# A transformer block on one core: full-height passes for the first gate and up products, and a planner that counts changes of TensorE's tile form

## The chip, the core and the metric

The kernel runs on one core of a Trainium2 chip. The core has five engines that run side by side and meet at semaphores: TensorE (PE in the profile, with its weight loads as PEld), VectorE (DVE), ScalarE (ACT), GpSimd (POOL) and SyncE (SP), which here does nothing but issue transfers. TensorE multiplies a stationary operand, which a weight load puts into its 128x128 array, with a moving operand, and accumulates into the eight banks of PSUM (128 partitions x 512 floats each). The metric is the device time of one execution in microseconds (us), lower is better.

## The reference

x is 2048 tokens of width 448, all in float32. The block is attention with a residual, then a gated feed-forward with a residual:

```python
h  = x + attention(layernorm(x)) @ wo        # 16 heads of 28, scale 28 ** -0.5,
                                             # a query sees itself and the 255 tokens before it
n  = layernorm(h)
h2 = h + (gelu(n @ w_gate) * (n @ w_up)) @ w_down   # 448 -> 1792 -> 448
```

## The kernel before, in words

**Precision.** Most products split each operand into a high part (rounded to the type that TensorE multiplies in one pass) and a low part, and add high x high, high x low and low x high: three passes for a product. ScalarE writes the high parts (`to_hi`), VectorE or GpSimd the low ones (`to_lo`).

**Attention.** There are 16 blocks B, each four heads by 512 queries. For a block, TensorE makes the scores (`scores`, L717), VectorE their row maxima, a small transpose brings the maxima to the keys' side (L748), TensorE makes the scores again transposed (`probs`, L792), ScalarE takes the exponential (L796), GpSimd zeroes what the window excludes (L811), TensorE multiplies with the values (`attend`, L830), `drain` normalises on VectorE and GpSimd, and after every second block `output` (L888) multiplies with wo. Query, key and value projections (L666, L612) of a later group of tokens lie between these steps. The last projections end during block 12, and blocks 13 to 15 are attention's tail.

**Feed-forward.** The 1792 hidden features are seven groups of 256 and the tokens two halves, which makes 14 pieces `m`. The first three pieces (CL = 3) are computed in the plain way, for two times 512 tokens and for gate and up each: twelve turns x = 0 to 11. The other eleven use a scheme of seven products in place of eight on halves of 64 contraction rows, and need no closer look here. All of it is issued as TensorE "slots": a slot is three pairs of passes, each pass on 64 of the 128 rows of the array, the two of a pair on the upper and the lower half at once, into two banks (`cslot` L1123 for the plain turns, `both` L1314 for the others, `down_half` L1388 for the product with w_down). In a plain turn the 448 contraction rows are three chunks of 128 and a rest of 64. `cslot(..., ph, j, banks)` takes half a chunk for each of the two output tiles: with ph = 0 the upper half for one tile and the lower half for the other, with ph = 1 the reverse; j = 3 is the rest. So a turn is three slots in `first` and four in `second`, 42 passes on half the rows. Between the two phases `seen` lets ScalarE read one element of a bank (L1234), which orders the two halves' writes into it. Turns 0 to 2 (kind "gu0", banks 5 and 6, named bank_177 and bank_178) may run while attention's tail is still at work, and turn 3 just after. The others come later.

**Three forms of the array.** In this text form 0 is a pass that uses the array as one piece (all of attention but `attend`, and `output`), form 1 is the pairs on 64 rows, and form 2 is `attend`, which uses four column strips of 32.

**What sets the order.** Nothing is written in the order in which it runs. Every step is an `op` with an engine, a cost, a latency, a key and the data that it reads and writes. `Lists.run` plans them: for each engine it looks for the steps that can start within a small margin of the earliest (EASE), takes the one with the lowest key (`choice`), and books its cost. The instructions stand in each engine's queue in the planned order, and each engine works its queue strictly in that order. The PSUM bank of a step is also given in the plan. All TensorE steps of the feed-forward are chained in program order (`queued`), so that the plan moves only what stands between them and what stands on the other engines. Some 50 constants at the top of the file enter keys: EVICT is how far an emptying of a bank is moved ahead, HASTE how far the splitting of w_down is, WLATE and XLATE how far back the weights and the second half of the tokens are put, XTIME in which half units of the feed-forward the three parts of those tokens are prepared, LAG_T, LAG_P and LAG_V how far maxima, probabilities and values trail the scores.

**Banks emptied.** `copied` and `added` (L1320, L1324) and the gelu of a plain turn (L1137) empty a bank of the feed-forward; a later slot that writes the same bank waits for that.

## Time and profile before

| | |
|---|---|
| median of 3 runs | 714.14 us (714.09 to 714.24) |
| the profiled execution | 714.1 us, its span 712.4 us |
| TensorE busy | 698.2 us, 98% of the span |
| VectorE, ScalarE, GpSimd busy | 75%, 58%, 44% |
| granted TensorE clock | 0.999 |
| first plain slot on TensorE; last `output` pass | 271.2 us; 329.2 us |

The span runs from the first to the last instruction; the time holds 1.7 us more, which lies around it. A row of the timeline merges neighbouring instructions of one kind: start, duration, engine, line, operation, output from input, rows used*columns, shape, and how many. Passes are pipelined: the recorded durations overlap, so what a row costs TensorE is best read from its start to the start of the next row.

### The profile page before, as it was taken

The page shows a single profiled execution, that of the slowest core. Times are in us where ns is not written, and L with a number is a line of the kernel's source. Part 1 is how long each engine was busy: PE and PEld are TensorE (multiplying, and loading weights), DVE is VectorE, ACT ScalarE, POOL GpSimd, SP SyncE. Part 2 cuts the span into 40 slices and gives each one's busy share as a digit, 9 for nine tenths or more (in the row PEclk, how much of TensorE's full clock was granted, in tenths as well). Part 3 has the DMA queues.
Part 4 walks back from the last instruction along what each step waited for, and adds up shares of the span by engine and source line. Part 5 has one row for each costly group of instructions (what it writes and reads, how often), then busy time and mean ns, then how long its engine had stood idle before and what let it go on. Part 6 is the DMA issues. An engine that isn't in the chain of part 4 may idle for free. (4 is left out here: it accounts for less than half of the span.)

```text
span 712.4 us, 15568 instructions
## 1 busy us (share of the span) xinstructions
PE 698.2 (98%) x5598; PEld 589.1 (83%) x5598; DVE 536.8 (75%) x1233; ACT 415.9 (58%) x917; POOL 312.7 (44%) x426
## 2 busy tenths in 40 slices
PE   8999999999999999999999999999999999999997
PEld 7887877787888876668787888788899999888996
DVE  7976779887787878838488678995755867877764
ACT  7748586876676675776454546645434545546431
POOL 5613553644465446441025876534403556556000
PEclk9999999999999999999999999999999999999999
DMA  8897967887778775305875866404303563443102
GB/s 310 271 289 208 276 169 192 223 233 212 190 182 250 212 225 143 95 12 129 231 190 172 233 188 190 133 18 135 90 4 109 175 191 114 131 156 87 41 14 104
DMA packets 104693, 116.27 MB, mean 163 GB/s; under 512 B 44632, under 2 KB 82392, under 8 KB 104040
## 3 DMA queue, kind: packets, MB, share of 16 engines
q1 hardware_dynamic: 104472, 115.17, 56.5%
q8 instruction: 44, 0.72, 0.4%
q14 instruction: 33, 0.27, 0.1%
q10 hardware_dynamic: 144, 0.11, 0.0%
HBM read 84.97 MB, written 44.47 MB: 182 GB/s over the span
## 5 line engine op out<-in xcount | busy, mean ns | idle before, releaser
L721 DVE CUSTOM_DVE_ANT_0 mt<-bank,mt 128x384 bf16<-128x384 f32 (+2 forms) x256 | 127.0, 527 | 32.3 <-PE bank L717 30.2
L796 ACT ACTIVATE pp<-bank 128x384 f32<-128x384 f32 (+1 forms) x212 | 105.2, 534 | 27.3 <-PE bank L792 18.0
L811 POOL TENSOR_SCALAR_AFFINE_SELECT pp<-pp 128x512 f32<-128x512 f32 x120 | 77.2, 658 | 86.1 <-ACT pp L796 83.8
L666 PE MATMUL bank<-xT 128*128 128x512 f32 x308 | 95.3, 400 | 0.0
L1314 PE MATMUL bank<-xT,proj 64*128 64x512 f32 x735 | 95.2, 388 | 0.0
L1314 PEld LDWEIGHTS bank<-xT,proj 64*128 64x128 f32 x735 | 77.7, 184 | 7.1 <-ACT raw L1320 0.2
L792 PE MATMUL bank<-rq,rk 104*128 104x384 f32 (+2 forms) x352 | 81.8, 307 | 0.7 <-ACT pp L796 0.6
L717 PE MATMUL bank<-rk,rq 84*128 84x384 f32 (+2 forms) x256 | 79.8, 342 | 0.7 <-DVE mx L721 0.7
L1388 PE MATMUL bank<-proj,gh 64*128 64x448 f32 x624 | 72.9, 363 | 2.0 <-ACT e L1234 2.0
L792 PEld LDWEIGHTS bank<-rq,rk 104*128 104x128 f32 x352 | 58.6, 189 | 15.8 <-ACT pp L796 6.9
L1388 PEld LDWEIGHTS bank<-proj,gh 64*128 64x128 f32 x624 | 61.7, 184 | 7.4 <-ACT e L1234 2.7
L1405 DVE TENSOR_TENSOR hres<-bank,hres 128x448 f32<-128x448 f32 (+1 forms) x113 | 62.9, 611 | 6.4 <-PE bank L1388 6.4
L1234 ACT ACTIVATE e<-bank 1x1 f32<-1x1 f32 x145 | 22.8, 157 | 68.0 <-PE bank L1388 48.0
L1183 POOL TENSOR_TENSOR xn<-proj 128x384 f32<-128x384 f32 (+1 forms) x36 | 37.2, 1039 | 56.6 <-DMA proj<-gu 42.9
L666 PEld LDWEIGHTS bank<-xT 128*128 128x128 f32 x308 | 55.6, 189 | 7.2 <-DVE proj L387 0.5
L717 PEld LDWEIGHTS bank<-rk,rq 84*128 84x128 f32 x256 | 46.7, 189 | 13.6 <-DVE mx L721 5.0
L1123 PE MATMUL bank<-xT,proj 64*128 64x512 f32 x420 | 53.5, 396 | 0.0
L384 ACT ACTIVATE rq<-bank 8x512 fp32r<-8x512 f32 x64 | 37.7, 589 | 26.2 <-PE bank L748 25.2
L1314 PE MATMUL bank<-xo,proj 64*128 64x512 f32 x366 | 48.5, 390 | 2.9 <-DVE v L1324 1.9
L387 DVE TENSOR_TENSOR proj<-proj 128x448 fp32r<-128x448 f32 (+2 forms) x42 | 31.0, 743 | 25.0 <-ACT proj L384 22.8
L612 PE MATMUL bank<-proj,xT 128*128 128x448 f32 (+1 forms) x220 | 48.0, 333 | 0.0
L1123 PEld LDWEIGHTS bank<-xT,proj 64*128 64x128 f32 x420 | 38.2, 184 | 10.4 <-issue 2.6
(175 smaller groups left out, 1420.7 us busy)
## 6 DMA issues: line engine op xcount, KB each, us to landing
rk<-k SPq DMA_DIRECT2D x44, 336.0 KB
rq<-q SPq DMA_DIRECT2D x32, 336.0 KB
gu<-in_gu_dram SPq DMA_DIRECT2D x18, 480.0 KB
proj<-gu SPq DMA_DIRECT2D x24, 288.0 KB
q<-proj SPq DMA_DIRECT2D x12, 448.0 KB
proj<-down SPq DMA_DIRECT2D x22, 224.0 KB
proj<-gu SPq DMA_DIRECT2D x24, 192.0 KB
k<-proj SPq DMA_DIRECT2D x9, 448.0 KB
```

The source lines that it names most:

```text
L384: nc.scalar.activation(dst, src, AF.Copy)
L612: op("pe", mm(224 * n), 0.29 if n == 1 else 0.38, key + a / 16, lambda a=a, h=h, wb=wb, xb=xb: nc.tensor.matmul(bank[b.k][:, 0:224 * n], x ...
L666: op("pe", mm(512) + 0.002, 0.403, key, lambda a=a, h=h, wb=wb, xb=xb: nc.tensor.matmul(bank[b.k], wqk[m][:, h, wb, :], xT[:, xb, cc * 128 ...
L717: nc.tensor.matmul(bank[b.k][:, o:384], rq[u][0:3 * DH, j, i * 128:i * 128 + 128], rk[u][0:3 * DH, j, m0 * 128:(i + 3) * 128], start=True, ...
L721: nc.vector.tensor_tensor_reduce(junk[s % 2][:, o:384], bank[b.k][:, o:384], mask[:, o:384], 1.0, -BIG, OP.add, OP.max, mx[:, i, j:j + 1])
L792: nc.tensor.matmul(bank[b.k][:, n * i:n * i + n], rk[u][0:104, j + i, m * 128:m * 128 + 128], rq[u][0:104, j + i, lo * 128:(hi + 1) * 128] ...
L796: nc.scalar.activation(pp[:, j:j + G, o * 128:o * 128 + n], bank[b.k][:, 0:G * n].rearrange("p (g t) -> p g t", g=G), AF.Exp, scale=SCALE)
L811: nc.gpsimd.affine_select(a, a, pattern=[[0, 4], [-cm, 128]], compare_op=op_, fill=0.0, base=0, channel_multiplier=cm)
L1123: nc.tensor.matmul(bank[banks[side ^ ph].k], cwbuf[n % 4][0]()[HALF[side], o:o + 128], carea(c, xl, j, side), start=not ph and not j and n ...
L1314: nc.tensor.matmul(bank[b.k], w, xarea(u.cp, xl, xs, side)[:, xk], start=p in (1, 2, 5) and not k and not t, stop=t == 2, tile_position=(6 ...
L1388: nc.tensor.matmul(bank[banks[q].k][:, 0:D], h[oh][0]()[HALF[x], q * 128:q * 128 + 128], d[wh][0]()[HALF[x]], start=not ph and not y and n ...
L1405: op("dve", 0.07 + w * 0.463 / D, 0.163 + w * 0.463 / D, key, lambda: nc.vector.tensor_tensor(hres[:, t, c0:c0 + w], bank[b.k][:, c0:c0 + ...
```

## The change

1. In turns 0, 1 and 2 (FULL = 3) the three chunks of 128 rows are no longer cut into halves. `cfull` makes three passes over all 128 rows into one bank, for each of three chunks and two output tiles: 18 passes in form 0 in the place of 36 on half the rows. The rest of 64 rows stays a `cslot` in form 1 (`range(3, 4)` in `second`), and the two `seen` of such a turn fall away. The other turns are as before.
2. Every step carries a `mode`, the form of its passes (0, 1 or 2). `choice` now plans a TensorE step whose form differs from that of the step before no earlier than TURN after TensorE comes free (0.19 for going to form 0, 0.09 for going to form 1 or 2). The delay is booked in the plan; which of the steps that could start goes first is still decided by the key.
3. The planned costs of `probs` and `attend` are altered, and 21 constants, which move steps in the plan; the first lines of the diff show those that matter below.

```diff
-EDGE = 9
+EDGE = 12
+FULL = 3
-XTIME = (6, 6, 8)
+XTIME = (6, 7, 8)
-XLATE = 0
-HASTE = 260
-WLATE = 65
+XLATE = 125
+XSTEP = 60
+HASTE = 300
+WLATE = 110
-XADD = ('dve', 'dve', 'dve', 'dve')
-XLO = ('dve', 'dve', 'dve', 'dve', 'pool')
+XADD = ('dve', 'pool', 'dve', 'dve')
+XLO = ('pool', 'dve', 'dve', 'dve', 'dve')
-EVICT = 15
+EVICT = 30
+TURN = (0.19, 0.09, 0.09)
...
-                    found.append((t, o, got))
+                    late = max(t, free[e] + TURN[o.mode]) if e == "pe" and o.mode != mode else t
+                    found.append((late, o, got, t))
...
-            return min((f for f in found if f[0] <= t0), key=lambda f: (f[1].key, f[0]))
+            return min((f for f in found if f[3] <= t0), key=lambda f: (f[1].key, f[0]))[:3]
...
-            cost = G * (n / 2400 + 0.009)
+            cost = G * max(n / 2400 + 0.009, 0.1)
...
-        cost = 0.33 + n * 0.214
-        op("pe", cost, cost + 0.2, 16 * B + LAG_P + ORDER[ms[-1]] + LAG_V, go, r, (), b, tag="att")
+        cost = 0.157 + n * 0.214
+        op("pe", cost, cost + 0.2, 16 * B + LAG_P + ORDER[ms[-1]] + LAG_V, go, r, (), b, tag="att", mode=2)
...
+        key0 = key
         for k in parts:
+            key = key0 + (0 if cp else XSTEP * k)
...
+    def cfull(key, n, c, k, i, banks):
+        reads = [t for l in range(2) for side in range(2)
+                 for t in (*cwtok(n, l, 384 * i + 128 * k, 128, side), *ctok(c, l, k, side))]
+
+        def go():
+            for t, (wl, xl) in enumerate(((0, 0), (0, 1), (1, 0))):
+                o = 896 * (1 - wl) + 384 * i + 128 * k
+                nc.tensor.matmul(bank[banks[i].k], cwbuf[n % 4][0]()[:, o:o + 128], carea(c, xl, k, 2),
+                                 start=not k and not t, stop=False, skip_group_check=True)
+        queued(op("pe", 0.7, 0.87, key, go, reads, (), banks[i]))
...
         def first(x):
             m, c, ty, banks = turns[x]
             key = ckey(x)
+            if x < FULL:
+                for j in range(6):
+                    cfull(key + j, 2 * m + ty, c, j // 2, j % 2, banks)
+                return
...
-            for b in banks:
-                seen(key, b)
-            for j in range(4):
+            if x >= FULL:
+                for b in banks:
+                    seen(key, b)
+            for j in range(0 if x >= FULL else 3, 4):
                 cslot(key + 2 * j, 2 * m + ty, c, 1, j, banks)
```

On TensorE, over block 15 in attention's tail, the plain slots of L1123 stood one at a time between single probability passes of L792 (bank_177 and bank_178 are the plain turns' banks, bank_174, 175 and 179 those of the probabilities; each pair of L1123 rows stands three times):

```order
L792 MATMUL bank_179<-rq_190,rk_188 128x384
L1123 MATMUL bank_178<-xT,proj 128x512
L1123 MATMUL bank_177<-xT,proj 128x512
...
L792 MATMUL bank_174<-rq_190,rk_188 128x384
L1123 MATMUL bank_178<-xT,proj 128x512
L1123 MATMUL bank_177<-xT,proj 128x512
...
L792 MATMUL bank_175<-rq_190,rk_188 128x384
L792 MATMUL bank_179<-rq_190,rk_188 128x384
```

In the changed kernel the same place on TensorE reads so, with L798 for the probabilities and L1143 for `cfull`:

```order
L798 MATMUL bank_179<-rq_190,rk_188 128x256 x2
L1143 MATMUL bank_177<-xT,proj 128x512 x3
L798 MATMUL bank_174<-rq_190,rk_188 128x256 x2
L1143 MATMUL bank_178<-xT,proj 128x512 x3
L798 MATMUL bank_175<-rq_190,rk_188 128x384
L798 MATMUL bank_179<-rq_190,rk_188 128x384
L1143 MATMUL bank_177<-xT,proj 128x512 x3
```

Three full passes now stand after each one or two probability passes, all in form 0. Counted over the whole of TensorE's queue, the form changes 94 times before and 70 times now: the separate stretches of form 1 ahead of the last `output` are 15 before and 3 now, and the visits to form 2 are 31 in both. From the last `output` passes on, the 3335 passes that follow are the same in the same order, with the same banks, to the end.

On ScalarE, at the end of a plain turn in the feed-forward (bank_174 and bank_175 hold its gate products, L1137 empties them with the gelu, L1234 is `seen`, the L384 rows split weights), before:

```order
L1234 ACTIVATE e_75<-bank_173 1x1
L384 ACTIVATE w_3388<-xn 128x384
L1137 ACTIVATE v<-bank_174 128x512
L384 ACTIVATE proj<-proj 128x448
L1137 ACTIVATE e_3390<-bank_175 128x512
L1234 ACTIVATE e_75<-bank_177 1x1
L1234 ACTIVATE e_75<-bank_179 1x1
```

and in the changed kernel, at the same turn on ScalarE (L1156, L1253 and L390 are the same three lines):

```order
L1156 ACTIVATE v<-bank_174 128x512
L1156 ACTIVATE e_3345<-bank_175 128x512
L1253 ACTIVATE e_75<-bank_177 1x1
L390 ACTIVATE w_3343<-xn 128x128
L1253 ACTIVATE e_75<-bank_179 1x1
L390 ACTIVATE w_3343<-xn 128x384
L390 ACTIVATE proj<-proj 128x448
```

The two emptyings now stand side by side, and the splits of weights behind them.

On VectorE, in a later unit of the feed-forward (L1324 empties a bank, L387 makes low parts, L1342 multiplies gate and up), before:

```order
L387 TENSOR_TENSOR w_3388<-xn,w_3388 128x384
L1342 TENSOR_TENSOR v<-raw,v 128x512
L1324 TENSOR_TENSOR v<-bank_172,v 128x512
L387 TENSOR_TENSOR e_3392<-v,e_3391 128x512
L1324 TENSOR_TENSOR v<-bank_175,v 128x512
```

and now, at the same unit on VectorE (L1361, L1343 and L393 are the same three lines):

```order
L1361 TENSOR_TENSOR v<-raw,v 128x512
L393 TENSOR_TENSOR w_3343<-w_3343 128x384
L393 TENSOR_TENSOR w_3343<-xn,w_3343 128x384
L393 TENSOR_TENSOR e_3347<-v,e_3346 128x512
L1343 TENSOR_TENSOR v<-bank_172,v 128x512
L1343 TENSOR_TENSOR v<-bank_175,v 128x512
```

The low part of the activation moved from between the two emptyings to ahead of both. Over the whole program ScalarE has 6 instructions fewer (the `seen` of three turns), VectorE 5 fewer and GpSimd 5 more (token preparation), and SyncE issues the same transfers.

More of the change, by code (lines that the diff above doesn't have):

```diff
@@ L93 @@
     __slots__ = ("eng", "cost", "lat", "key", "fn", "deps", "users", "left", "banks", "port", "ready", "start", "fin",
-                 "size", "tag")
+                 "size", "tag", "mode")
 class Bank:
@@ L109, in __init__, with op @@
         self.ops, self.seen, self.open, self.all = [], {}, {}, {}
-    def op(self, eng, cost, lat, key, fn, r=(), w=(), bank=None, port=False, size=0, tag=None, after=(), part=None):
+    def op(self, eng, cost, lat, key, fn, r=(), w=(), bank=None, port=False, size=0, tag=None, after=(), part=None, mode=0):
         o = Op()
-        o.eng, o.cost, o.lat, o.key, o.fn, o.port, o.size, o.tag = eng, cost, lat, key, fn, port, size, tag
+        o.eng, o.cost, o.lat, o.key, o.fn, o.port, o.size, o.tag, o.mode = eng, cost, lat, key, fn, port, size, tag, mode
         o.deps, o.users, o.ready, o.start = set(after), [], 0.0, None
@@ L221, in run @@
                 dmas.append(t + lat)
-            if e == "pe" and t < SLOW:
-                cost, lat = 2 * cost, lat + cost
+            if e == "pe":
+                mode = o.mode
+                if t < SLOW:
+                    cost, lat = 2 * cost, lat + cost
             free[e] = t + cost
@@ L1315, in go @@
                                      stop=t == 2, tile_position=(64 * side, 0), skip_group_check=True)
-        queued(op("pe", 0.69, 0.86, key, go, reads, (), [x[3] for x in two]))
+        queued(op("pe", 0.69, 0.86, key, go, reads, (), [x[3] for x in two], mode=1))
     def copied(key, buf, b):
@@ L1393, in down_half @@
             queued(op("pe", 3 * mm(D), 3 * mm(D) + 0.17, key + j, lambda j=j: go(j, h, d), [h[0][1], h[1][1], *d[0][1], *d[1][1]], (),
[L1394 removed]
+                      [banks[2 * j], banks[2 * j + 1]], mode=1))
             if not ph:
```

31 lines of the change are left out of this document (15 added, 16 removed).

## The prediction

> **What bounds the kernel.** I read the page first, then the chain of waits, then busy time by stretch.
>
> ```profile
> span 712.4 us, 15568 instructions
> PE 698.2 (98%) x5598; PEld 589.1 (83%) x5598; DVE 536.8 (75%) x1233; ACT 415.9 (58%) x917; POOL 312.7 (44%) x426
> ...
> PE 27%; DVE 1%; issue 0%; DVEq 0%
> ```
>
> TensorE is busy for 98% of the span, and the chain that ended last is nearly all TensorE. So the time is the sum of what TensorE issues, and I look for two things: passes that cost more than they should, and waits that the busy share hides because pipelined passes overlap. The stretches below show TensorE's busy time in the first number after the comma; the stretch's length minus that is idle time.
>
> ```profile
> 296.00:329.00 33.00, 32.66 (x263) 23.13 (x262) 18.16 (x45) 23.75 (x49) 12.15 (x19) 1.00 0.13 30
> 329.00:360.00 31.00, 30.07 (x263) 24.40 (x263) 20.22 (x38) 15.01 (x39) 4.53 (x9) 1.00 0.82 206
> 360.00:400.00 40.00, 38.93 (x354) 33.42 (x352) 31.34 (x54) 20.11 (x54) 18.33 (x16) 1.00 0.71 191
> 400.00:440.00 40.00, 37.99 (x338) 33.36 (x337) 34.20 (x48) 24.10 (x59) 27.48 (x27) 1.00 0.71 208
> 440.00:480.00 40.00, 39.02 (x352) 33.45 (x351) 37.96 (x56) 20.61 (x51) 20.54 (x18) 1.00 0.31 90
> 520.00:560.00 40.00, 40.00 (x368) 36.99 (x366) 23.68 (x36) 16.17 (x40) 9.74 (x10) 1.00 0.31 90
> ```
>
> From 329 to 480 us TensorE idles 0.9 + 1.1 + 2.0 + 1.0 = 5.0 us; from 520 to 560 none. In attention's tail (296 to 329) it hardly idles, so a gain there must come from the passes themselves. The timeline of the tail, start by start, shows where:
>
> ```profile
> 291.67 0.96 PE L1123 MATMUL bank<-xT,proj 64*128 64x512 f32 x6
> 292.56 0.45 PE L717 MATMUL bank<-rk,rq 84*128 84x384 f32 x1
> 292.85 0.34 PE L792 MATMUL bank<-rq,rk 104*128 104x384 f32 x1
> 293.12 0.97 PE L1123 MATMUL bank<-xT,proj 64*128 64x512 f32 x6
> 294.02 0.79 PE L792 MATMUL bank<-rq,rk 104*128 104x384 f32 x3
> ...
> 295.32 0.69 PE L717 MATMUL bank<-rk,rq 84*128 84x384 f32 x3
> 295.85 0.40 PE L792 MATMUL bank<-rq,rk 104*128 104x384 f32 x1
> ...
> 315.61 2.33 PE L1123 MATMUL bank<-xT,proj 64*128 64x512 f32 x18
> 317.87 1.50 PE L830 MATMUL bank<-pp,v 128*29 128x384 f32 x24
> 319.30 5.08 PE L1123 MATMUL bank<-xT,proj 64*128 64x512 f32 x42
> 324.31 5.22 PE L888 MATMUL bank<-proj,ohl 128*128 128x448 f32 x24
> ```
>
> A stretch of 18 half-row passes (9 pairs) lasts 317.87 - 315.61 = 2.26 us, one of 42 (21 pairs) 324.31 - 319.30 = 5.01. Twelve pairs more cost 2.75, so a pair costs 0.229 and three pairs 0.69. But three pairs alone last 292.56 - 291.67 = 0.89, and again 294.02 - 293.12 = 0.90: a stretch of form 1 pays 0.20 beside its passes. The form-0 stretch behind it pays too: two passes of 384 columns last 293.12 - 292.56 = 0.56, while three of them in a row last 295.85 - 295.32 = 0.53, 0.177 each; 0.56 - 2 x 0.177 = 0.21. So one visit to form 1 and the way back cost about 0.40 us, more than half of the slot's own 0.69.
>
> **The skill on this.** "Mode switching requires drain: Changing tiling mode (not just tile) drains the TensorE", says the Trainium skill, TensorEngine Tiling (Array Packing), Key Properties. The trace agrees: some 0.2 us at each change. The Trainium skill, TensorE: Matmul & The Clock Gate, Single matmul latency, puts the drain at about 175 ns; with that, 24 changes would be an estimated 4.2 us where my rows give 4.8.
>
> **Part 1, form changes.** By the order of TensorE's queue, 94 changes become 70: twelve of the fifteen separate stretches of form 1 in the tail are gone, each with its way back. 24 x 0.20 = 4.8 us, all on TensorE, which is the bound there. Visits to form 2 stay at 31, so their cost stays.
>
> **Part 1, passes.** 54 pairs of half-row passes become 54 passes over all rows. What such a pass costs shows at the projections, which have the same 512 columns in form 0:
>
> ```profile
> 31.78 2.48 PE L666 MATMUL bank<-xT 128*128 128x512 f32 x10
> 34.10 0.38 PE L612 MATMUL bank<-proj,xT 128*128 128x224 f32 x2
> ...
> L666 PEld LDWEIGHTS bank<-xT 128*128 128x128 f32 x308 | 55.6, 189 | 7.2 <-DVE proj L387 0.5
> ```
>
> Ten last 34.10 - 31.78 = 2.32 us, 0.232 each, against 0.229 for a pair: 54 x 0.003 = +0.2 us. The time of the passes is nearly the same, so nothing else is saved. The six `seen` that go are ScalarE work beside TensorE and count nothing; banks 5 and 6 are still emptied once a turn.
>
> **Part 2, order in the feed-forward.** TensorE's order is unchanged there, so a gain or loss can only be a wait. Each of the idle times above is a bank emptied late. One of about 1 us, with both engines in one timeline:
>
> ```profile
> 379.37 1.37 PE L1388 MATMUL bank<-proj,gh 64*128 64x448 f32 x12
> ...
> 379.73 0.53 ACT L384 ACTIVATE w<-xn 128x384 fp32r<-128x384 f32 x1 [1.89 <-POOL xn L1183]
> 380.16 0.58 ACT L1137 ACTIVATE v<-bank 128x512 f32<-128x512 f32 x1
> 380.64 0.57 ACT L384 ACTIVATE proj<-proj 128x448 fp32r<-128x448 f32 x1
> 381.11 0.59 ACT L1137 ACTIVATE e<-bank 128x512 f32<-128x512 f32 x1
> 381.58 0.34 ACT L1234 ACTIVATE e<-bank 1x1 f32<-1x1 f32 x2
> 381.78 0.47 PE L1388 MATMUL bank<-proj,gh 64*128 64x448 f32 x2 [1.03 <-ACT e L1234]
> ```
>
> TensorE waits at 381.78 for `seen`, which stands behind two emptyings, which stand behind a weight split that waits for GpSimd, and with another split between them. In the new queue the two emptyings come first and the splits behind. The banks are full at about 379.5, two emptyings and a `seen` take 0.5 + 0.5 + 0.2, so `seen` ends near 380.8, when TensorE is done with L1388 (379.37 + 1.37): the 1.03 us go. What is late next are the splits of weights that were ahead, by about 1 us; the rows show no pass waiting for them there. A second one is on VectorE:
>
> ```profile
> 424.97 0.69 DVE L1324 TENSOR_TENSOR v<-bank,v 128x512 f32<-128x512 f32 x1 [2.53 <-PE bank L1314]
> ...
> 425.35 1.39 PE L1388 MATMUL bank<-proj,xT 64*128 64x448 f32 x12
> 425.58 1.44 DVE L387 TENSOR_TENSOR e<-v,e 128x512 fp32r<-128x512 f32 x1
> ...
> 426.94 0.68 DVE L1324 TENSOR_TENSOR v<-bank,v 128x512 f32<-128x512 f32 x1
> ...
> 427.67 0.50 PE L1314 MATMUL bank<-xo,proj 64*128 64x512 f32 x2 [0.93 <-DVE v L1324]
> ```
>
> The low part of 1.44 us stood between two emptyings. Now it stands ahead of both, where VectorE idled 2.53 us; the second emptying follows at 425.6, and the 0.93 us go. Together -1.9 us. The idle 0.9 us of the row for 329 to 360 stays: ScalarE's rows there are the same. In the other reordered places the cost is unknown; a new order can make further waits of this size, or remove some. Bounds -3.1 (all the rest of the 5.0 goes) to +3 (three new ones of 1 us); I take +1.0, one new wait of the size seen, since two such waits shown were a matter of one row's place.
>
> **Part 3, order in attention.** The moved keys (LAG_T, EDGE and the like) shift work that TensorE does anyway. What they can change is again waits. In the tail such a wait looks like this one, for an exponential:
>
> ```profile
> 312.54 0.89 PE L792 MATMUL bank<-rq,rk 104*128 104x384 f32 x3 [0.34 <-ACT pp L796]
> ```
>
> I take 0, with bounds of three such waits less (-1) and six more (+2).
>
> **The sum.** -4.8 + 0.2 - 1.9 + 1.0 + 0 = -5.5 us. The profiled execution took 714.1, its span 712.4 and 1.7 around it; the median of the runs is the same to 0.1. So 714.1 - 5.5 = 708.6 us. With the bounds of the last two parts: from 708.6 - 4.1 - 1 = 703.5 to 708.6 + 2 + 2 = 712.6; for this case I call 705.5 to 711.5 likely, since the ends do not come together.
>
> **The rivals.** *The tail turns to ScalarE's pace.* If TensorE gets ahead by 4.8 us, it may only wait longer for exponentials. The row for 296 to 329 shows ScalarE busy 23.75 of 33 us, while a block's exponentials are
>
> ```profile
> L796 ACT ACTIVATE pp<-bank 128x384 f32<-128x384 f32 (+1 forms) x212 | 105.2, 534 | 27.3 <-PE bank L792 18.0
> ```
>
> 212 / 16 = 13 a block at 0.5 us each, 6.6 us. For it: full passes now stand as filler after every two probability passes, 3 x 0.232 = 0.7 us against two exponentials' 1.0. Two probability passes add 0.35, which makes TensorE's cycle 1.05 and the two even. Against: ScalarE itself waited 18.0 us for L792 over the run. If half to all of the 4.8 came back as waits, the time would be 711 to 713.4.
>
> *Tokens for the second half come late (slower).* XLATE and XTIME put one third of these tokens' preparation half a unit back. The unit that first reads them, and the last of their preparation:
>
> ```profile
> L1314 PE MATMUL bank<-xo,w x222: 386/392/507, 388.3 to 515.8; 64*128 64x512 f32 x111
> L1314 PE MATMUL bank<-xT,proj x735: 383/386/466, 474.4 to 689.9; 64*128 64x512 f32 x184
> ...
> 472.78 1.62 POOL L387 TENSOR_TENSOR xT<-v,xT 64x512 fp32r<-64x512 f32 x1 [3.69 <-ACT xT L384]
> ```
>
> Three units lie between 388.3 and 474.4, 28.7 us each, so half a unit is 14.3. The preparation already ended just at its use. Were it half of that late, TensorE would stand for 7.2 us: 708.6 + 7.2 = 715.8, and above 5.5 us the change loses. Against it: with the third go nine loads, four differences and seven splits on three engines, but in the new queues of ScalarE and VectorE these rows stand no further back against the emptyings near 470 us than before, and the order of SyncE's transfers there is all but the same.
>
> *Weight loads no longer hide.* A pass on one half of the rows could load its weights while the other half worked. If each full pass paid its 0.189 us, 54 would cost 10.2: 708.6 + 10.2 = 718.8. The row of L666 speaks against it: 0.232 a pass with a load of 0.189 for each. The Trainium skill, TensorE: Matmul & The Clock Gate, Part 3, has this as a rule: loads overlap with passes under way "only when row_grp differs". By that rule the change is slower; L666 contradicts it.
>
> *The planner does not gather the slots.* Excluded by the order, which shows 70 changes.
>
> **Chances.** The forecast with its range 705.5 to 711.5: 0.70. Better than that: 0.05. The tail at ScalarE's pace: 0.11, half of it below 712.7. Late tokens or weights: 0.11. Weight loads: 0.01. No difference for other reasons: 0.02. This kernel's runs lie within 0.02%, but I call less than 0.2% (1.4 us) no change. Faster: 0.70 + 0.05 + 0.06 = 0.81; within 0.2%: 0.05 + 0.02 = 0.07; slower 0.12. The range for 8 in 10 reaches from 705.5 into the second rival's end: 713.0.
>
> **What would show it.** Right: single slots' 0.89 us gone from the tail, with L1143's three passes lasting 0.70 and the probabilities behind them 0.177 each; last `output` 4 to 6 us earlier; no TensorE wait of 1 us at the plain turn that was at 381 or at the unit that was at 427. Wrong: waits of TensorE for L802's exponentials over 3 us in the tail, a gap ahead of the first pass on the second half's tokens, or more than two new late emptyings between 330 and 520 us.

## The result

The changed kernel takes 709.8 us (median of 20 runs, 707.9 to 713.9), the kernel before on the same chip 714.1 (20 runs, 713.3 to 716.0). The ratio is 0.9942, 95% interval 0.9929 to 0.9956: faster by 4.3 us. The forecast was 708.6 us, with 705.5 to 713.0 around it. The profiled execution took 710.2 us, its span 708.5.

The head of the page of the changed kernel:

```profile
span 708.5 us, 15457 instructions
...
PE 695.2 (98%) x5544; PEld 587.3 (83%) x5544; DVE 534.5 (75%) x1228; ACT 414.7 (59%) x911; POOL 318.6 (45%) x431
```

TensorE is still the bound, with 54 passes fewer and 3.0 us less of busy time. Busy time in the same stretches as before (length, then the busy times of TensorE, its weight loads, VectorE, ScalarE and GpSimd; the 1.00 or 0.96 is TensorE's granted clock as a share of full speed, and the last two numbers are of the transfers):

```profile
296.00:329.00 33.00, 33.00 (x242) 24.71 (x241) 17.54 (x39) 22.26 (x44) 8.91 (x14) 1.00 0.22 49
329.00:360.00 31.00, 30.07 (x268) 24.62 (x266) 22.12 (x41) 17.39 (x42) 10.50 (x13) 1.00 0.84 225
360.00:400.00 40.00, 38.99 (x350) 32.04 (x346) 31.68 (x46) 19.29 (x55) 24.24 (x24) 1.00 0.73 206
400.00:440.00 40.00, 38.20 (x324) 34.13 (x326) 33.66 (x46) 21.43 (x55) 26.37 (x25) 0.96 0.62 184
440.00:480.00 40.00, 39.73 (x356) 34.02 (x354) 35.38 (x57) 21.50 (x52) 20.71 (x14) 1.00 0.27 79
```

From 329 to 480 us TensorE now idles 0.9 + 1.0 + 1.8 + 0.3 = 4.0 us, against 5.0. And one thing is new: between 400 and 440 the clock is 0.96 of full speed.

The timeline of TensorE in the tail of the changed kernel (start, duration, line):

```profile
303.92 0.86 PE L1143 MATMUL bank<-xT,proj 128*128 128x512 f32 x3
304.62 0.51 PE L798 MATMUL bank<-rq,rk 104*128 104x384 f32 x2
304.97 0.84 PE L1143 MATMUL bank<-xT,proj 128*128 128x512 f32 x3
...
305.92 0.97 PE L1131 MATMUL bank<-xT,proj 64*128 64x512 f32 x6
306.81 0.80 PE L798 MATMUL bank<-rq,rk 104*128 104x384 f32 x3
...
316.09 4.38 PE L1131 MATMUL bank<-xT,proj 64*128 64x512 f32 x36
320.39 5.13 PE L894 MATMUL bank<-proj,ohl 128*128 128x448 f32 x24
325.46 3.70 PE L1131 MATMUL bank<-xT,proj 64*128 64x512 f32 x30
```

Three full passes last 304.62 - 303.92 = 0.70 us, and the two probability passes behind them 304.97 - 304.62 = 0.35: no extra, as the form stays. A slot of form 1 that is still alone lasts 306.81 - 305.92 = 0.89, as before. The last `output` is over at 325.46, where it was at 329.45 before:

```profile
329.45 1.89 PE L1123 MATMUL bank<-xT,proj 64*128 64x512 f32 x14
```

By then the changed kernel has 12 half-row passes fewer left to do. Behind the last `output` of the changed kernel its trace has 3333 passes, two fewer than was said with the change. Counted back from the end, so that each of them is set against the same pass of the kernel before, the changed kernel is ahead by 331.40 - 326.03 = 5.4 us near the first of them, and by 3.9 at the end. So 1.5 us are given back in the feed-forward.

The timeline of TensorE shows where (in brackets the idle time just before a row, and who ended it). Its rows are the plain turn that waited 1.03 us before, the two waits that lie closest together, and the unit after 426 us.

```profile
379.57 2.60 PE L1407 MATMUL bank<-proj,gh 64*128 64x448 f32 x24
...
398.52 1.08 PE L1407 MATMUL bank<-proj,gh 64*128 64x448 f32 x8 [0.61 <-DVE proj L393]
400.62 3.71 PE L1333 MATMUL bank<-xo,proj 64*128 64x512 f32 x18 [1.02 <-ACT e L1253]
404.13 1.63 PE L1407 MATMUL bank<-proj,gh 64*128 64x448 f32 x12
...
429.40 1.40 PE L1407 MATMUL bank<-proj,xT 64*128 64x448 f32 x10 [0.79 <-DVE xT L393]
```

The plain turn at 379.57 runs through in one row of 24 passes: its wait is gone. But 18 passes from 400.62 last 404.13 - 400.62 = 3.51 us, where 9 pairs at 0.229 would be 2.06. The granted clock (the third number from the end) in these stretches:

```profile
397.83:401.25 3.42, 1.79 (x16) 1.21 (x16) 3.42 (x4) 1.44 (x6) 3.19 (x4) 1.00 0.87 286
401.25:404.66 3.41, 3.41 (x20) 2.72 (x18) 1.75 (x3) 1.30 (x3) 0.63 (x1) 0.50 0.37 99
404.66:408.07 3.41, 3.41 (x35) 3.00 (x32) 1.07 (x3) 1.29 (x3) 3.12 (x3) 1.00 0.39 115
```

The clock stands at one half for 3.41 us, from 401.25 to 404.66, which costs 1.7 us of work: right behind two waits of 0.61 and 1.02 us. The second of them is not new. In the kernel before it stands alone, and the clock stays at 1.00 behind it:

```profile
406.13 0.73 PE L1314 MATMUL bank<-xo,proj 64*128 64x512 f32 x4 [1.02 <-ACT e L1234]
```

So the one new wait, of 0.61 us, stands close ahead of an old one, and the fall follows. This was not in the prediction. The Trainium skill, TensorE: Matmul & The Clock Gate, Part 1, gives the clock two states, full and half, and a free-running window of 3413 ns by which the gate decides; the length of the fall agrees with it, but here no idle time of a whole window was needed.

### The profile page after: what moved, and what is told of

It reads as the page before. It is cut to its first block, busy times and chain, and to the rows that moved or that the text cites. A ratio compares the mean times of both kernels' runs of the same rounds, so it can differ in the third digit from the quotient of the medians.

```text
span 708.5 us, 15457 instructions
## 1 busy us (share of the span) xinstructions
PE 695.2 (98%) x5544; PEld 587.3 (83%) x5544; DVE 534.5 (75%) x1228; ACT 414.7 (59%) x911; POOL 318.6 (45%) x431
## 4 chain that ended last, share of the span: by engine, by line
PE 89%; DVE 6%; ACT 2%; issue 1%; DMA 1%; POOL 1%; DVEq 0%; ACTq 0%
PE bank L1333 24%; PE bank L1407 17%; PE bank L672 9%; PE bank L798 7%; PE bank L723 7%; PE bank L1131 7%; PE bank L836 6%; PE bank L894 5%; PE bank L618 5%; PE bank L1143 2%; DVE xT L393 1%; DVE hres L1424 1%; DVE proj L393 1%; DVE v L1343 1%; PE bank L448 0%
## 5 line engine op out<-in xcount | busy, mean ns | idle before, releaser
L802 ACT ACTIVATE pp<-bank 128x384 f32<-128x384 f32 (+1 forms) x212 | 104.4, 534 | 27.1 <-PE bank L798 18.0
L1333 PE MATMUL bank<-xT,proj 64*128 64x512 f32 x735 | 94.9, 388 | 0.0
L1333 PEld LDWEIGHTS bank<-xT,proj 64*128 64x128 f32 x735 | 75.8, 184 | 9.1 <-DVE v L1343 0.3
L798 PE MATMUL bank<-rq,rk 104*128 104x384 f32 (+2 forms) x352 | 82.1, 306 | 0.5 <-ACT pp L802 0.4
L798 PEld LDWEIGHTS bank<-rq,rk 104*128 104x128 f32 x352 | 58.9, 189 | 15.0 <-ACT pp L802 4.5
L1253 ACT ACTIVATE e<-bank 1x1 f32<-1x1 f32 x139 | 21.8, 157 | 74.9 <-PE bank L1407 52.7
L1202 POOL TENSOR_TENSOR xn<-proj 128x384 f32<-128x384 f32 (+1 forms) x36 | 34.1, 952 | 56.1 <-DMA proj<-gu 36.0
L393 DVE TENSOR_TENSOR proj<-proj 128x448 fp32r<-128x448 f32 (+2 forms) x42 | 34.2, 820 | 24.5 <-ACT proj L390 23.9
L390 ACT ACTIVATE rq<-bank 8x512 fp32r<-8x512 f32 x64 | 37.6, 588 | 21.3 <-PE bank L754 20.2
L836 PE MATMUL bank<-pp,v 128*29 128x384 f32 (+2 forms) x704 | 45.2, 388 | 0.0
L1333 PEld LDWEIGHTS bank<-xo,proj 64*128 64x128 f32 x366 | 38.5, 189 | 7.2 <-ACT e L1253 1.6
```

The source lines that it names most:

```text
L798: nc.tensor.matmul(bank[b.k][:, n * i:n * i + n], rk[u][0:104, j + i, m * 128:m * 128 + 128], rq[u][0:104, j + i, lo * 128:(hi + 1) * 128] ...
L802: nc.scalar.activation(pp[:, j:j + G, o * 128:o * 128 + n], bank[b.k][:, 0:G * n].rearrange("p (g t) -> p g t", g=G), AF.Exp, scale=SCALE)
L836: nc.tensor.matmul(bank[b.k][32 * j:32 * j + DH + 1, lo * 128:(hi + 1) * 128], v[:, at_v(4 * c - 2 + m), 4 * g + j, :], pp[:, j, at[m] * 1 ...
L1333: nc.tensor.matmul(bank[b.k], w, xarea(u.cp, xl, xs, side)[:, xk], start=p in (1, 2, 5) and not k and not t, stop=t == 2, tile_position=(6 ...
```

## The experiments

Four questions: is 0.20 us per change of form a price or a coincidence; which part of the change earns the gain; is the half clock caused by the waits; and how much waiting it takes.

### The price of a change, in another place

```diff
-        for q, c0, w in [(q, 0, D) for q in range(3)] + [(3, 0, D // 2), (3, D // 2, D // 2)]:
+        for q, c0, w in [(q, 0, D) for q in range(3)] + ([(3, 0, D // 2), (3, D // 2, D // 2)] if m == 13 else [(3, 0, D)]):
...
-            out_add(key + 3 * q + 1, m, c, q, banks[q], c0, w)
+            out_add(key + 3 * q + 1 if m == 13 else key - OUTK + q // 2, m, c, q, banks[q], c0, w)
...
-                    if m == 13 and not c and y:
+                    if (m == 13 and not c or 7 <= m <= 11) and y:
```

> The kernel before, with one edit in the feed-forward: for pieces 7 to 11 the second half of the product with w_down is done in passes over all 128 rows (form 0), 120 of them, instead of 120 pairs on half the rows. The passes cost the same in time; the form changes 20 times more (94 to 114), each time amid work that never waited before 520 us and later. Theory 1 (every change of form costs TensorE 0.20 us): 714.1 + 20 x 0.20 = 718.1 us, and in the trace about 0.2 us too much at each edge of such a stretch. Rival (the 0.2 us belong to attention's neighbours, such as weight loads of the 104-row passes, and not to the change of form): 714.1 +- 0.5 us.

Measured: 721.3 us, ratio 1.0102 (1.0089 to 1.0115). One of the ten new stretches on TensorE (L1421 is the product in form 0, between slots in form 1):

```profile
565.05 2.73 PE L1421 MATMUL bank<-proj,gh 128*128 128x448 f32 x12
567.72 2.34 PE L1314 MATMUL bank<-xT,proj 64*128 64x512 f32 x18
```

The 12 passes last 567.72 - 565.05 = 2.67 us. In the changed kernel, 24 passes of that shape (L894 at 320.39) take 5.07 with their own change, so a pass is at most 0.211 and by the difference 0.200: 12 are 2.4 to 2.5, and some 0.2 are left for the change. With the way back, the ten visits cost 0.39 each in the trace, 3.9 us together for 20 changes. That is the predicted price, far from attention. The total is 3 us above what Theory 1 gave. Some 2.3 of them are five waits for ScalarE's `seen` (the weight load stands 0.51 us at 570.36, and as long at 598.83, 627.41, 655.66 and 684.18), which are not there before; each sets TensorE back by 0.45. They stand behind the new stretches, where 12 passes in a lump may leave ScalarE less time; the rest of the 3 us was not traced.

### Each part alone

Five kernels take away the full passes, the count of changes, or the constants (the planned costs of item 3 stay with the count of changes, and with the price at 0 too; XSTEP = 0 and TURN = 0 are the code before).

The count alone, with the old constants and no full passes:

```diff
-FULL = 3
+FULL = 0
...
-XLATE = 125
-XSTEP = 60
-HASTE = 300
+XLATE = 0
+XSTEP = 0
+HASTE = 260
...
```

> The changed kernel with the constants of before and FULL = 0: no full passes, only the planner's booking of form changes (TURN) and the two altered planned costs. 74 changes of form instead of 94. Theory 1: 20 x 0.20 = 4.0 us less in attention's tail; with the waits of before in the feed-forward 710.1 us, 708.5 to 712. Rival (the gain comes from the new constants, which take waits away): 713.5 to 714.5 us.

Full passes alone, in the code before:

```diff
+FULL = 3
+XSTEP = 0
+TURN = (0.0, 0.0, 0.0)
...
```

> The kernel before with the full passes alone (FULL = 3), constants and planned costs of before and TURN = 0. 72 changes of form instead of 94. Theory 1: 22 x 0.20 = 4.4 us less, 54 full passes 0.2 more: 709.9 us, 708.5 to 712. Rival (constants): 713.5 to 714.5 us.

Full passes and count, with the 21 old constants:

```diff
-EDGE = 12
+EDGE = 9
...
-XLATE = 125
-XSTEP = 60
+XLATE = 0
+XSTEP = 0
...
```

> The changed kernel with the 21 constants of before: full passes, TURN and the altered planned costs stay. 70 changes of form as in the changed kernel. Theory 1: 24 x 0.20 = 4.8 less, 0.2 more: 709.5 us if the feed-forward waits as before, so that the new constants are worth nothing in the median. If the constants carried part of the gain by fewer waits: 711 to 713 us. And on the clock: the changed kernel's runs spread from 707.9 to 713.9 us, with a lower clock after two waits within 3 us near 400 us; if the new constants make that pair of waits, this kernel's runs lie closer together, within 2 us.

All but the full passes:

```diff
-FULL = 3
+FULL = 0
```

> The changed kernel with all its constants, but without the full 128-row passes: 82 changes of form in place of 70, and 54 more passes. Theory (0.20 us a change, 0.2 us for the full passes together): attention's tail ends 12 x 0.20 - 0.2 = 2.2 us later than in the changed kernel; 711 to 712.5 us, if the feed-forward's waits stay the same. Rival (passes of full rows cost as much as they save, and the gain lies in the order): 709.5 to 710.3. Other rival (without them the tail's order comes apart, as with the old constants): over 716.

All but the price of a change:

```diff
-TURN = (0.19, 0.09, 0.09)
+TURN = (0.0, 0.0, 0.0)
```

> The changed kernel with full passes and all its constants, but with a change of form priced at nothing in the list (three numbers set to 0). The list still comes to 70 changes of form: the full passes alone take them away. Theory after the other runs (full passes carry the gain; what the price of a change does is a choice between orders, and each order brings waits of its own): attention's excess over plain passes falls by 4.8 us as in the changed kernel, and the time is 709 to 714, according to the waits that the new order has. Rival (the price is what makes the order good): over 715, with waits in the stretch 270 to 300 as in the runs with the old constants. Other rival (the price does nothing): 709.8.

The column "first plain" has the start of the first plain pass on TensorE, "ahead" how far the profiled execution is ahead of the kernel before at the first plain passes that both issue alike behind attention (minus: behind).

| full passes | count | new constants | changes | first plain, us | ahead, us | median us | ratio (95%) |
|---|---|---|---|---|---|---|---|
| no | no | no | 94 | 271.2 | 0 | 714.1 | 1 |
| yes | no | no | 72 | 269.9 | 5.7 | 716.3 | 1.0022 (1.0011 to 1.0033) |
| no | yes | no | 74 | 298.0 | -12.3 | 727.0 | 1.0186 (1.0168 to 1.0204) |
| yes | yes | no | 70 | 292.3 | -9.4 | 723.4 | 1.0125 (1.0112 to 1.0139) |
| no | yes | yes | 82 | 283.4 | -1.8 | 717.0 | 1.0045 (1.0029 to 1.0060) |
| yes | price 0 | yes | 70 | 288.5 | -6.9 | 723.8 | 1.0136 (1.0119 to 1.0153) |
| yes | yes | yes | 70 | 272.5 | 5.4 | 709.8 | 0.9942 (0.9929 to 0.9956) |

All five are slower than the kernel before, and none came out in the range that its theory gave. Two fit a rival that was on record: all but the full passes (over 716) and all but the price (over 715, with waits between 270 and 300 us). All 21 constants alone, and the two planned costs alone, were not run. The number of changes alone decides nothing: 70 changes stand at 709.8, at 723.4 and at 723.8. What goes with the end of attention is when the first plain pass comes: in the four kernels where it stands at 283 us or later, attention ends behind the kernel before, and the later the further.

*Full passes alone* earn somewhat more than their forecast of 4.2 us: at the later plain slots the kernel is ahead by 5.7 us, 0.7 of it by shorter waits in the tail. Then 8 us are given back in the old feed-forward order, mostly in waits. The worst, on TensorE:

```profile
370.10 0.50 PE L1131 MATMUL bank<-xT,proj 64*128 64x512 f32 x1
372.82 6.70 PE L1131 MATMUL bank<-xT,proj 64*128 64x512 f32 x41 [2.22 <-DVE v L1171]
```

Behind it 41 half-row passes last 379.13 - 372.82 = 6.3 us in place of 4.7 (20.5 pairs at 0.229): half clock again, for 3.4 us.

*The count with the old constants* leaves TensorE with little but attention's own steps in the stretch from 270 to 300 us, because the plain slots come late. The row of that stretch, of the run with the count alone:

```profile
270.00:300.00 30.00, 26.61 (x143) 16.28 (x142) 22.69 (x75) 18.74 (x40) 15.98 (x29) 0.77 0.31 85
```

143 passes, 3.4 us idle, and a clock of 0.77; the first plain slot comes at 298.0 (271.2 before). In the changed kernel the same stretch is

```profile
270.00:300.00 30.00, 29.88 (x235) 21.07 (x235) 28.03 (x89) 22.10 (x46) 17.68 (x28) 1.00 0.51 141
```

with 235 passes and 0.1 us of idle time, because the first full passes stand at 272.5. It is not simply that a half-row slot costs a change and so is put off: with the count and the old constants the full passes, which cost no change there, stand as late as 292.3. Why the plan comes out so was not shown; the runs show that all three parts together bring the first plain pass to 272.5 and keep the gain.

*Without the full passes*, the rest kept, I had expected twelve changes less 54 x 0.003 of passes, 2.2 us. It is 7.2. The first later plain passes are 7.2 us later than in the changed kernel, too: 2.4 by the twelve changes, 2.7 by waits of TensorE that the trace shows between 270 and 326 us, and some 2 that were not traced to a cause. Three of the waits:

```profile
282.94 0.28 PE L754 MATMUL bank<-one,mhl 128*104 128x128 f32 x1 [0.75 <-DVE mhl L747]
...
283.38 0.96 PE L1131 MATMUL bank<-xT,proj 64*128 64x512 f32 x6
...
306.51 1.65 PE L798 MATMUL bank<-rq,rk 104*128 104x384 f32 x6 [0.39 <-ACT pp L802]
...
318.25 2.16 PE L1131 MATMUL bank<-xT,proj 64*128 64x512 f32 x12 [0.69 <-ACT v L1339]
```

The first slot stands at 283.4, eleven us after the first full pass of the changed kernel. Until then TensorE waits for maxima (0.75) and exponentials; later the `seen` between halves and the emptyings hold it up. So the rival "the tail turns to ScalarE's pace" is in part real here. It does not belong to the half-row slots alone: *with the price at nothing* the plain passes are full ones, the first stands at 288.5, one waits 1.32 us for its weights (L393) at 290 us, TensorE waits for maxima (0.89) and exponentials (0.79) too, the idle time of the stretch is 3.3 us, and its clock 0.89.

### The feed-forward's constants

The changed kernel with eleven of the constants set back (XTIME, XLATE, XSTEP, HASTE, OUTK, WLATE, XADD, XLO, HOLDD, EVICT, LNLATE), and the kernel before with the same set forward, but for XSTEP, which it does not have:

```diff
-XLATE = 125
-XSTEP = 60
-HASTE = 300
-OUTK = 80
-WLATE = 110
+XLATE = 0
+XSTEP = 0
+HASTE = 260
+OUTK = 60
+WLATE = 65
...
```

> The changed kernel, with the constants that bear on the feed-forward (transposition times, lateness of splits, who makes which split, how late the residual sums go) as they were before; those of attention, the full passes and the count of changes stay. Theory (attention's end gains 5.3 us by the passes and attention's constants; the feed-forward's order then decides by itself how much is kept): attention's tail ends 5 us earlier as in the changed kernel, and the feed-forward's waits come out anew. If the new feed-forward constants were worth the 1.9 us that the prediction gave them, this kernel takes 711.5 to 712; if their order only swaps some waits for others (as the changed kernel's ledger says, two of 1.0 gone and three of 0.8 come), 709 to 710.5. Rival (the old feed-forward constants don't fit the earlier end, as in the run with full passes alone, which gave 8 us back there): 714 or more, with a fall of the clock behind a cluster of waits.

```diff
-XTIME = (6, 6, 8)
+XTIME = (6, 7, 8)
...
-XLATE = 0
-HASTE = 260
-OUTK = 60
-WLATE = 65
+XLATE = 125
+HASTE = 300
+OUTK = 80
+WLATE = 110
...
```

> The kernel before, with the feed-forward's constants of the changed kernel; no full passes, no count of changes, attention's constants as before. Theory (attention's gain comes from the form changes): the tail ends within 2 us of the kernel before (86 changes of form in place of 94: at most 1.6 us earlier by 0.20 each), and the feed-forward swaps waits: 713 to 715. Rival (the new feed-forward order carries a good part of the 4.3 us gain): 711.5 to 712.5.

Measured: 718.8 us, ratio 1.0063 (1.0044 to 1.0082), and 718.9, ratio 1.0063 (1.0046 to 1.0080). The first has the time of its rival (714 or more) but not its reason, which was an earlier end of attention; the second misses both. In both, attention itself comes out otherwise: their first plain pass stands at 283.7 and 277.5, and at the first of the like passes they are 4.8 and 5.1 us behind the kernel before, again with a cluster of waits between 285 and 294 us and 6.8 us at half clock with it. So the constants do not split into a group for attention and a group for the feed-forward; that this is because VectorE and ScalarE serve both in one queue each is likely, and not shown. What the feed-forward's order is worth by itself these two runs do not tell; that stays open.

### The half clock

At 394.94 us VectorE makes four additions to the residual ahead of the split that TensorE waits for at 398.52. They are cut to one column each, so that 447 of 448 columns of these sums are left out; every engine's order stays.

```diff
-                out_add(key - OUTK + q // 2, m, c, q, banks[q])
+                out_add(key - OUTK + q // 2, m, c, q, banks[q], seen=1 if (m, c) == (1, 1) else D)
...
-            hres[:, t, c0:c0 + w], bank[b.k][:, c0:c0 + w], hres[:, t, c0:c0 + w], op=OP.add)
+            hres[:, t, c0:c0 + min(w, seen)], bank[b.k][:, c0:c0 + min(w, seen)], hres[:, t, c0:c0 + min(w, seen)], op=OP.add)
```

> The changed kernel, with the four VectorE additions to the residual at 394.94 us (2.21 us together, just ahead of the split that TensorE waits for at 398.52) cut to one column each; the order of every engine is unchanged. Left out: 447 of 448 columns of that part's sum. Theory (two TensorE waits close together, 0.61 us at 398.52 and 1.02 us at 400.62, bring the granted clock to one half at 401 to 405, and this makes the changed kernel's runs spread from 707.9 to 713.9): the split then starts when ScalarE's half of it is done, at 396.1, and the first wait is gone; the second shrinks to about 0.75; a single wait is left there, the clock stays at 1.0, and the pairs at 401 to 405 cost 0.23 and not 0.43 us. Times 707 to 707.6 us, all runs within about 1 us. Rival (the clock falls there for another reason, such as the work done up to then): the waits go, which is worth 0.9 us, and the half clock at 401 to 405 stays: median 708.9, with the spread of the changed kernel.

Measured: 708.9 us (707.1 to 709.6, 6 runs), ratio 0.9919 (0.9904 to 0.9934). TensorE's timeline of this run, and the stretch in which the clock had fallen:

```profile
362.36 1.48 PE L1407 MATMUL bank<-proj,xT 64*128 64x448 f32 x12 [1.32 <-ACT e L1253]
...
398.98 1.37 PE L1407 MATMUL bank<-proj,gh 64*128 64x448 f32 x12
401.21 2.34 PE L1333 MATMUL bank<-xo,proj 64*128 64x512 f32 x18 [0.86 <-ACT e L1253]
```

```profile
400.00:404.00 4.00, 3.14 (x28) 2.36 (x26) 3.94 (x5) 2.08 (x7) 3.61 (x3) 1.00 0.82 251
```

The turn at 398.98 is one row of 12 passes, one wait of 0.86 is left, the clock stays at 1.00, and the row of 18 passes lasts 2.34 us in place of 3.71. Between 397 and 405 us the kernel gains 2.6 us on the changed one. With one of the two waits gone the fall is gone, as the theory has it. One execution does not rule out the rival, a fall for another reason, because a kernel can have the fall in one execution and not in another; the runs below bear on that. That the median is the 708.9 which the rival gave, and not the 707 to 707.6 of the theory, has another reason in the profiled execution: 1.3 us go at 362.36, to a wait that the changed kernel's profile does not have. ScalarE's rows there, of this run:

```profile
360.15 0.63 ACT L390 ACTIVATE xo<-xo 64x512 fp32r<-64x512 f32 x1 [2.59 <-DMA xo<-xn]
...
361.21 1.05 ACT L1156 ACTIVATE v<-bank 128x512 f32<-128x512 f32 x2
362.16 0.34 ACT L1253 ACTIVATE e<-bank 1x1 f32<-1x1 f32 x2
```

and of the changed kernel:

```profile
357.72 0.63 ACT L390 ACTIVATE xo<-xo 64x512 fp32r<-64x512 f32 x1 [0.48 <-DMA xo<-xn]
```

ScalarE's queue stands still for a transfer of tokens that landed 2.4 us later in the one execution than in the other, and the emptying and `seen` that TensorE needs stand behind it. The program is the same up to there, so this is a difference between executions. It is one reason why the runs spread: I had expected one us, and it is 2.5.

To see how much waiting brings the clock down, the split that TensorE waits for at 428 us was issued twice and three times, in the kernel with the small additions.

```diff
-            o.fn()
+            [o.fn() for _ in range(2 if e == 'dve' and o.key == 1796.0 and 425 < t < 426 else 1)]
```

> The kernel with the four small additions, and VectorE's split of the tile that TensorE waits for at 428.2 us (0.79 us of idle, alone in its neighbourhood) issued twice, so that the wait there grows by one split of 0.94 us to about 1.7 us. Theory (the clock falls when waits of together 1.6 us or more lie within 3 us, not for one wait of about 1 us): this one lies at the boundary; if the sum of idle time decides, the clock falls at about 430 to 434 and the time is 0.9 + 1.7 us more than with the small additions alone; if it takes two waits, the clock stays at 1.0 and the time is 0.9 us more. Either is a result: it tells sum from cluster.

> The same with that split issued three times: the wait at 428.2 grows to about 2.7 us. If the sum of idle time within some 3 us decides, the clock falls for sure: 1.9 + 1.7 to 2 us more than with the small additions alone. If it takes two waits, the clock stays at 1.0 and the time is 1.9 us more.

Measured: 708.7 us (707.2 to 710.4), ratio 0.9927 (0.9913 to 0.9941), and 711.2 us (710.6 to 711.7), ratio 0.9963 (0.9950 to 0.9975). TensorE with the split issued twice, and the clock around it:

```profile
428.43 1.40 PE L1407 MATMUL bank<-proj,xT 64*128 64x448 f32 x10 [2.19 <-DVE xT L393]
```

```profile
424.34:427.76 3.42, 1.90 (x17) 1.35 (x13) 3.38 (x6) 2.40 (x6) 1.94 (x2) 1.00 0.88 254
427.76:431.17 3.41, 2.74 (x24) 2.69 (x26) 3.41 (x6) 1.55 (x4) 1.31 (x2) 1.00 0.78 211
```

and issued three times:

```profile
429.23 2.24 PE L1407 MATMUL bank<-proj,xT 64*128 64x448 f32 x10 [2.91 <-DVE xT L393]
431.26 4.04 PE L1333 MATMUL bank<-xo,w 64*128 64x512 f32 x18
```

```profile
425.17:428.58 3.41, 1.15 (x11) 0.64 (x7) 3.34 (x5) 1.66 (x5) 2.00 (x2) 1.00 0.88 258
428.58:432.00 3.42, 2.77 (x14) 2.48 (x16) 3.42 (x6) 0.92 (x4) 1.28 (x1) 0.50 0.71 200
432.00:435.41 3.41, 3.41 (x18) 2.67 (x18) 3.30 (x2) 1.19 (x3) 3.33 (x4) 0.50 0.21 61
```

The first step grew the wait by 1.4 us, not 0.9, since a split took 1.2 there; the median did not rise over the 708.9 of the small additions alone, whose profiled execution had the extra 1.3 us at 362 (these two kernels ran on another chip). One wait of 2.19 us leaves the clock at 1.00; one of 2.91 halves it for 6.83 us, two pieces of 3.41. The extra 0.7 us of waiting brought 2.5 us in the medians.

Why 2.19 us did not do it, while 2.22 did in the run with full passes alone and 0.61 + 1.02 did in the changed kernel, the traces show when they are cut as the rows above are. In every trace of this case all changes of the granted clock lie whole multiples of 3.41 us apart: each execution has its own fixed grid of windows, and the clock changes only at their edges. What counts is TensorE's idle time inside one window. In the changed kernel both waits lie in the window from 397.83 to 401.25, with 3.42 - 1.79 = 1.63 us idle. With full passes alone the whole 2.22 us lie in one window. With the split issued twice the edge at 427.76 cuts the wait into 1.5 and 0.7 us, and neither window brings a fall; issued three times, 2.26 us lie in one. Between 329 and 520 us, over all thirteen traces, these three are the only windows with more than 1.60 us of idle time, and the only ones with a fall behind them; one with 1.60, with full passes alone, had none:

```profile
394.23:397.64 3.41, 1.81 (x17) 1.22 (x15) 1.70 (x2) 2.66 (x6) 3.18 (x4) 1.00 0.80 224
397.64:401.05 3.41, 2.29 (x24) 1.67 (x20) 2.94 (x4) 1.07 (x4) 2.37 (x3) 1.00 1.00 258
```

That fits the free-running window of the Trainium skill's page named above. In attention the border lies elsewhere, since there falls stand behind windows with only 0.3 to 1.6 us of recorded idle time; the recorded ends of short passes may hide idle time there, and this stays open. Where the grid lies differs between executions, so the same waits bring a fall in one and not in another: the two waits of the changed kernel stretch over 400.62 - 397.91 = 2.71 of 3.41 us, so if both have to lie in one window, an estimate from these numbers is that one execution in five has the fall. The six runs with the split issued twice fall into two groups, 707.2 to 707.8 and 709.6 to 710.4; the mean clocks on record are 0.998 and 0.999 in the first, and 0.996, 0.997 and 0.999 in the second, so a fall fits two of the slower three. With the split issued three times four of the five runs have 0.995 or 0.996. So the waits as the cause of the falls are well supported for the feed-forward: one more split, and nothing else, brought them.

## Why the prediction was right, and where it was not

**Part 1, form changes and passes: right.** Predicted -4.8 + 0.2 = -4.6; measured -5.4 at the first of the like passes, of which Part 3 is -0.9, which leaves -4.5. The price held in another place too (0.39 a visit). L1143's three passes last 0.70, the probabilities behind them 0.35 for two, and the last `output` ended 4.0 us earlier, at the lower edge of the 4 to 6.

**Part 3, order in attention: taken as 0, it was about -0.9.** From 100 us to the last `output`, TensorE's waits for maxima and exponentials fell from 1.4 us in four waits to one of 0.4 at 135 us; in the tail, from 255 us on, they fell from 1.2 us to none. It lies inside the bound of -1 that the prediction gave. That it hung on constants, count and full passes together was not seen: with any one of the three taken from the changed kernel, the first later plain passes come 7 to 15 us later.

**Part 2, order in the feed-forward: the sign was wrong.** Both named waits are gone as predicted: -1.0 at the plain turn that was at 381, and -1.2 at the unit that was at 427. The 0.9 us near 350 stayed. The failed step is "I take +1.0, one new wait". In its place stand +3.7: by the comparison of the like passes, +0.8 at 398, +1.6 at 401 to 405, +0.7 at 425 to 430, +0.9 at 436 to 438 and +0.7 at 444 to 446, less 0.8 at 453 and 0.2 in small steps. Five places for one, and among them the half clock, a term that the sum did not have at all. The bound of +3 was too small as well, in this execution.

**The sum** came out near, in part by luck, for two errors that partly cancel: 0.8 us better in attention, 2.4 worse in the feed-forward (-2.2 + 3.7 = +1.5 in place of -0.9). 708.6 - 0.8 + 2.4 = 710.2, the profiled time. That is the account of one execution. Of the twenty runs, six lie at 707.9 to 708.4, nine at 709.3 to 710.6, with nothing between, and five above. The step has about the size of one fall, but falls do not explain it: one fall of 3.41 us makes the mean clock 0.998, and the runs at 709.88, 709.92, 710.56 and 711.32 us have 1.000 on record. The lowest clocks, 0.997 and 0.995, stand at three of the four slowest runs (712.2 to 713.9). What else parts the runs is open; the late transfer at 357 us is one candidate. One reading of the prediction was thinner than it says: the chain of the page before is "nearly all TensorE", but covers 28% of the span; that TensorE is the bound rests on its 98% of busy time.

**The rivals.** ScalarE's pace: out for this kernel (0.4 us of waits for L802 in all, none of it in the tail), but waits of this kind came as soon as the full passes, the price or the new constants were taken away. Late tokens: not at the units that the rival named, where no wait above 1 us stands; at 357 us, for other tokens, ScalarE does wait for a transfer, 0.5 us in one execution and 2.6 in another. Weight loads: out, since three passes take 0.70 us with 0.188 us of load each:

```profile
L1143 PEld LDWEIGHTS bank<-xT,proj x54: 186/188/192, 272.4 to 315.5; 128*128 128x128 f32 x54
L1143 PE MATMUL bank<-xT,proj x54: 388/393/500, 272.5 to 315.8; 128*128 128x512 f32 x54
```

## What to carry to other kernels

A change of TensorE's array form has a price that can be read off two stretches of different length, and a full-height pass costs the same as a pair of half-height ones; so filler between steps should be in the form of its neighbours. When a stage ends earlier, look at what the stages behind it were fitted to: here the passes alone earned 5.7 us and lost 8, and only together with a new order did 4.3 remain. And price a wait not by its length alone: two waits of 0.6 and 1.0 us close together cost 1.6 us more in the profiled execution, because both fell into one window of 3.41 us and the clock fell behind it.

## What the hardware showed that was not expected

The granted clock of TensorE changes only at the edges of windows of 3.41 us, whose place differs from one execution to the next. In the feed-forward it fell to one half for a window, or two, behind windows with 1.63, 2.22 and 2.26 us of idle time, and not behind one with 1.60; a wait of 2.19 us that an edge cut in two brought no fall.

A split on VectorE takes more than twice as long in one place as in another. Two of the same line and shape in the changed kernel, with what GpSimd does beside the first:

```profile
397.07 1.39 DVE L393 TENSOR_TENSOR proj<-proj 128x448 fp32r<-128x448 f32 x1
427.87 0.60 DVE L393 TENSOR_TENSOR proj<-proj 128x448 fp32r<-128x448 f32 x1
...
395.86 2.12 POOL L1202 TENSOR_TENSOR xn<-xn,proj 64x384 f32<-64x384 f32 x2
398.06 1.27 POOL L393 TENSOR_TENSOR proj<-xn,proj 128x384 fp32r<-128x384 f32 x1
...
428.19 0.60 POOL L393 TENSOR_TENSOR proj<-xn,proj 128x128 fp32r<-128x128 f32 x1 [3.46 <-ACT proj L390]
```

The slow one has GpSimd at work all the while; beside the fast one GpSimd starts only at 428.19. Of the 0.61 us that TensorE waits at 398.52, these 0.79 us are more than all. Over the changed kernel's trace, the eleven splits of this line and shape with GpSimd idle beside them take 0.62 to 0.63 us, the others 0.56 to 2.5. That GpSimd is the cause is what the rows suggest; no run took it away.
